# Softmax sums of the tokens as 128x8 distinct values, and an output projection split into 384 and 128 columns, in a recurrent-memory attention kernel

## The chip, the cores and the metric

The kernel runs on one core of a Trainium2 chip. A core has five engines with instruction queues of their own: TensorE (matrix products, PE in the profile; its weight loads are shown apart as PEld), VectorE (DVE), ScalarE (ACT), GpSimd (POOL) and SyncE (SP), which in this kernel only issues DMA transfers. Matrix products are written to PSUM, eight banks of 128 partitions by 512 fp32 values; everything else lives in SBUF or DRAM. The metric is the device time of one execution in microseconds, as the median of several runs. Beside it stands one profiled execution, from which all durations are read.

## The reference

A gated mix of two branches over 2048 tokens of width 512. Branch B is a layer norm with a two-layer MLP. Branch A is attention with a recurrent memory and is where the change lies: the tokens are cut into 64 segments of 32, and each segment is attended together with 8 memory rows, which the segment before has made.

```python
idx = jnp.arange(L)                                    # L = M + seg = 8 + 32
mask = (idx[:, None] < M) | (idx[:, None] >= idx[None, :])
mem = mem0
for s in range(n_seg):                                 # 64
    xs = x[:, s * seg_len:(s + 1) * seg_len, :]
    h = jnp.concatenate([mem, xs], axis=1)
    q = jnp.einsum('btd,dhe->bhte', h, Wq)             # 32 heads of 128
    k = jnp.einsum('btd,dhe->bhte', h, Wk)
    v = jnp.einsum('btd,dhe->bhte', h, Wv)
    scores = jnp.einsum('bhqe,bhke->bhqk', q, k) * scale
    p = _softmax(jnp.where(mask[None, None], scores, -1e9), axis=-1)
    o = jnp.einsum('bhqk,bhke->bhqe', p, v)
    o = jnp.einsum('bhte,hed->btd', o, Wo)
    mem = o[:, :M, :]
    outs.append(o[:, M:, :])
a = jnp.concatenate(outs, axis=1)
return g * a + (1 - g) * b                             # g = sigmoid((x * gate_w).sum(-1))
```

## The kernel before

The first 100 us run branch B over all tokens, keep its result `c` in DRAM and load the weights of branch A. Then 64 steps `s`, one per segment, run in an order written out by hand; every engine executes its queue in the order of the program. `T, si = divmod(s, 4)`: four segments make a tile of 128 tokens.

A step works on 32 rows, the 8 memory rows and the first 24 tokens of its segment (`hT`); the last 8 tokens of each segment (LEFT) don't depend on the memory as queries, keys and values, and are projected for a whole tile at a time, as side work. Products of 32 rows use a quarter of the array's columns, so four of them, at the four column tiles, run side by side.

What a step issues, in TensorE's order:

- q and k (L110, banks `U[0]` to `U[3]`; cast by ScalarE at L115, transposed by VectorE at L119), a mask added to the score banks `Sb[0]` (in bank `SbF`) and `Sb[1]` (in bank `W`) at L248, scores of heads 0 to 15 (L256, L260), v (L129, banks `X1`, `X2`), scores of heads 16 to 31.
- The exponentials (L661, ScalarE) write `E`: for each of 8 groups i of 4 heads, 56 columns per key row, of which 0 to 15 belong to the 8 memory queries (they come twice), 16 to 47 to the 32 token queries, and 48 to 55 to the left tokens' keys for the last 8 of these queries. The key rows of four heads j lie in four blocks of 32 partitions.
- The sums over keys for the memory queries (`msum`, L267 and L270), their reciprocal (L668) and the product with E (L669, VectorE, two SBUF operands) are needed at once: attention times V (`av`, L280 and L285) reads E after it, in two halves.
- The sums for the token queries (`sums` with `xsum`, L693): the ones-blocks `BO` are the weights and E moves, so that each sum comes out on 32 partitions alike, 256 columns in `SbF`.
- `recip_x` (L603): VectorE inverts those 256 columns; SP sends four partitions of them to DRAM (`r_dr`, L606) and reads them back onto all 128 partitions (`Rb`, L607, 4 KB per partition); GpSimd adds the inverse to a running check (`racc`, L608).
- After `av`, ScalarE copies the memory columns to `UT` (L697) and the unnormalized token columns to `XR` (L598). In the next step GpSimd multiplies `XR` by `Rb` (`x_norm`, L614 and L615) into the columns 8 to 31 of `UT` and into `UL`. So the tokens of a segment are projected one step later than its memory rows: `wo_pass` in step s projects the memory rows of s and the tokens of s - 1.
- `wo_pass` (L618): eight groups of four matmuls (L141, 512 columns) into bank `W`, then ScalarE's copy to `w` (L622). Then a mask (L248), some side work, and the four matmuls that pick and transpose the memory rows of `w` (L709, 128 columns of `w` each). VectorE copies them to the next step's `hT` (L710), and the next q and k wait for that.

`fill` is the side work, handed out in pieces of four matmuls by `run(n)`: two pieces before the token sums (W1), two after `av` (W2), two after `wo_pass` (W3), the rest after L709. By si it is the next tile's left q and k (0 and 1), the last tile's left output (2) or left v (3); `extra` adds an output selection for si 0 and a transposition for si 3, between W3 and L709. `flush` runs pending copies in VectorE's and ScalarE's queues.

GpSimd's queue in a step: the next `hT` copy (L239), `x_norm` of the step before (it waits for Rb), `racc`, `prep_q` (L243); once in four steps the copy `GL` (L163). SP's queue: the loads of `c`, `VP` and `xs`, the two transfers of `recip_x`, the output. After the loop, the last step's sums, projection and check.

Of the kernel before, what the change touches and what calls it, by code (L numbers as in the profile page):

```python
# [27 lines left out]
def kernel(ctx, tc, A_x, A_mem0, A_Wq, A_Wk, A_Wv, A_Wo, A_seg_len, B_x, B_w1, B_b1, B_w2, B_b2, gate_w, out):  # L28
# [36 lines left out]
    r_dr = [dram.tile([4, 32 * NG], FP32, name=f"r_dr{i}") for i in range(2)]  # L65
# [71 lines left out]
    def wo_group(bk, U_, n):  # L137
        j, ih = HORD[n]
        for c in range(4):
            i = 4 * ih + c  # L140
            nc.tensor.matmul(bk[32 * c:32 * c + 32, :], lhsT=U_[:, j, i, :], rhs=Wo_sb[:, 4 * i + j, :],  # L141
                             start=(n == 0), stop=(n == NW - 1), tile_position=(0, 32 * c))
# [451 lines left out]

    def x_raw(s):
# [5 lines left out]
    def recip_x(s):  # L601
        R = Rs.pop(s)
        nc.vector.reciprocal(out=R[:, 8 * NG:], in_=SbF[:, 0:32 * NG])  # L603

        Rb = cw.tile([P, 4, NG, 32], FP32, tag="Rb", bufs=1, name="Rb")
        nc.sync.dma_start(r_dr[s % 2][:], R[0:P:32, 8 * NG:])  # L606
        nc.sync.dma_start(Rb[:].rearrange("p j i q -> p (j i q)"), r_dr[s % 2][:].rearrange("j f -> (j f)").partition_broadcast(P))  # L607
        nc.gpsimd.tensor_tensor(out=racc[:], in0=racc[:], in1=R[:], op=ALU.add)  # L608
        Rbs[s] = Rb

    def x_norm(s):
        T, si = divmod(s, SPT)
        XR, Rb = XRs.pop(s)[:].rearrange("p j i q -> p (j i) q"), Rbs.pop(s)[:].rearrange("p j i q -> p (j i) q")
        nc.gpsimd.tensor_tensor(out=UT[(s + 1) % 2][:].rearrange("p j i q -> p (j i) q")[:, :, M:32], in0=XR[:, :, 0:RIDE], in1=Rb[:, :, 0:RIDE], op=ALU.mult)  # L614
        nc.gpsimd.tensor_tensor(out=UL[T % 2][:].rearrange("p j i q -> p (j i) q")[:, :, LEFT * si:LEFT * si + LEFT],  # L615
                                in0=XR[:, :, RIDE:32], in1=Rb[:, :, RIDE:32], op=ALU.mult)

    def wo_pass(U_):  # L618
        for n in range(NW):
            wo_group(W, U_, n)  # L620
        w = cw.tile([P, Dm], BF16, tag="w", bufs=8, name="w")
        nc.scalar.copy(out=w[:], in_=W[:])  # L622
        return w

    W1, W2, W3 = 2, 2, 2
    for s in range(nseg):
# [56 lines left out]
        for i2 in range(2):  # L683
            exps(1, i2)
        for kc in range(2, KC):
# [7 lines left out]
        sums(xsum, E, 16, 48, 32, True)  # L693
# [18 lines left out]
        nc.vector.tensor_tensor(out=rmin[:], in0=rmin[:], in1=R[:], op=ALU.min)  # L712
# [166 lines left out]
```

## Time and profile before

| what | us |
|---|---|
| median of 3 runs | 796.58 |
| lowest, highest run | 795.5, 797.68 |
| profiled execution | 799.87 |
| its span, from the first to the last record | 798.1 |
| TensorE busy in the span | 774.5 (97%) |
| ScalarE busy | 529.9 (66%) |
| VectorE busy | 444.0 (56%) |
| GpSimd busy | 260.4 (33%) |

The granted clock of TensorE was 0.999 of full speed. Rows of the grouped view read: line, engine, operation, output <- inputs, shapes, count | busy us, mean ns of one | idle time of the engine just before, with what ended it. Rows of a timeline read: start us, us, engine, line, operation, count, and in brackets the idle time before. Rows of the chain of work that ended last read: start us, us, what. Rows of the waits read: engine, line, tile <- what it waited for: us in total, times, longest. Matmuls are pipelined: a row's duration includes the tail of its last matmul (0.17 us), during which the next one already runs.

### The profile page before, as it was taken

To read this page: it belongs to the slowest core of one execution; us is meant where nothing else is said; L and a number is where in the kernel's file an instruction comes from. 1 tells how busy PE (TensorE), PEld (TensorE's weight loads), DVE (VectorE), ACT (ScalarE), POOL (GpSimd) and SP (SyncE) were. 2 spreads that over 40 slices of the span, in tenths; PEclk is the share of its full clock that TensorE was granted. 3 is DMA by queue.
4 is the path that set the end of the run, shared out by engine and by line. 5 is a ranking of instruction groups with operands and counts; after the bars stand their busy time and mean duration, and the time that the engine had idled before them with its cause. 6 is when DMAs were issued, how large, how long until landed. Compare 5 with 4: busy or idle time off the path is not lost.

```text
span 798.1 us, 41399 instructions
## 1 busy us (share of the span) xinstructions
PE 774.5 (97%) x18446; PEld 421.2 (53%) x18446; DVE 444.0 (56%) x1061; ACT 529.9 (66%) x1440; POOL 260.4 (33%) x391
## 2 busy tenths in 40 slices
PE   7999999999999999999999999999999999999996
PEld 5666554555555555555554555555555555555543
DVE  4776355555556454646555555655465556555554
ACT  3666676666666676666666667767666766666663
POOL 3111033333343333243343334333334333333331
PEclk9999999999999999999999999999999999999999
DMA  6779411212112222212121211222221212121211
GB/s 188 264 273 351 134 57 60 73 59 86 60 53 68 76 69 76 70 49 67 60 86 60 86 49 62 70 76 70 70 76 53 64 60 86 60 80 60 66 47 57
DMA packets 38151, 70.42 MB, mean 88 GB/s; under 512 B 3979, under 2 KB 27888, under 8 KB 36432
## 3 DMA queue, kind: packets, MB, share of 16 engines
q1 hardware_dynamic: 36448, 64.97, 24.5%
q8 instruction: 146, 2.39, 1.2%
q0 software_dynamic: 720, 1.97, 0.7%
q10 hardware_dynamic: 800, 0.79, 0.3%
q14 instruction: 37, 0.30, 0.1%
HBM read 59.06 MB, written 4.45 MB: 80 GB/s over the span
## 4 chain that ended last, share of the span: by engine, by line
PE 92%; ACT 3%; DVE 2%; issue 1%; DMA 1%; POOL 0%; DVEq 0%; POOLq 0%; ACTq 0%
PE U L110 28%; PE X L129 17%; PE W L141 14%; PE X L110 6%; PE U L468 5%; PE U L280 4%; PE X L141 3%; ACT w L622 3%; PE W L462 3%; PE SbF L462 3%; PE W L709 1%; PE U L267 1%; DVE E L669 1%; PE SbF L256 1%; PE W L248 1%
## 5 line engine op out<-in xcount | busy, mean ns | idle before, releaser
L115 ACT CAST Tb<-U 128x512 bf16<-128x512 f32 x258 | 151.2, 586 | 81.3 <-PE U L110 80.8
L614 POOL TENSOR_TENSOR UT<-XR,Rb 128x768 bf16<-128x768 bf16 x63 | 104.7, 1662 | 239.8 <-DMA Rb<-r_dr 214.6
L110 PEld LDWEIGHTS <-hT 128*32 128x32 bf16 x4096 | 103.7, 97 | 109.9 <-DVE hT L710 19.1
L110 PE MATMUL U<-Wq_sb,hT 128*32 128x512 bf16 x2048 | 132.7, 379 | 1.1 <-DVE hT L710 1.1
L129 PE MATMUL X<-Wv_sb,hT 128*32 128x512 bf16 x2048 | 133.5, 378 | 0.0
L110 PE MATMUL U<-Wk_sb,hT 128*32 128x512 bf16 x2048 | 132.7, 379 | 0.0
L141 PE MATMUL W<-Wo_sb,UT 128*32 128x512 bf16 x2080 | 124.3, 380 | 1.2 <-ACT UT L697 1.2
L608 POOL TENSOR_TENSOR racc<-racc,R 128x320 f32<-128x320 f32 x63 | 54.5, 866 | 181.1 <-DVE R L603 176.5
L603 DVE RECIPROCAL R<-SbF 128x256 f32<-128x256 f32 x63 | 110.3, 1751 | 0.0
L119 DVE STREAM_TRANSPOSE QT<-Tb 128x256 f32<-128x256 f32 x128 | 57.0, 446 | 74.2 <-ACT Tb L115 74.1
L119 DVE STREAM_TRANSPOSE KT<-Tb 128x256 f32<-128x256 f32 x128 | 57.0, 445 | 54.9 <-ACT Tb L115 54.9
L141 PEld LDWEIGHTS <-UT 128*32 128x32 bf16 x2080 | 56.3, 96 | 58.5 <-issue 20.0
L710 DVE CAST hT<-W 128x32 bf16<-128x32 f32 x63 | 12.1, 192 | 132.8 <-PE W L709 132.8
L598 ACT CAST XR<-U 128x256 bf16<-128x256 f32 x252 | 78.4, 434 | 0.0
L622 ACT CAST w<-W 128x512 bf16<-128x512 f32 x65 | 38.1, 586 | 44.8 <-PE W L141 44.8
L697 ACT CAST UT<-U 128x64 bf16<-128x64 f32 x252 | 35.3, 226 | 46.7 <-PE U L285 46.7
L668 DVE RECIPROCAL R<-U 128x32 f32<-128x32 f32 x126 | 44.9, 357 | 25.7 <-PE U L270 24.2
L129 PEld LDWEIGHTS <-hT 128*32 128x32 bf16 x2048 | 45.4, 95 | 20.6
L468 PE MATMUL U<-w_sb,hTm 128*128 128x512 bf16 (+1 forms) x176 | 53.0, 385 | 0.0
L115 ACT CAST Tb<-X 128x512 bf16<-128x512 f32 x62 | 36.5, 589 | 18.0 <-PE X L110 18.0
L462 PEld LDWEIGHTS <-w_sb 128*128 128x128 bf16 (+1 forms) x352 | 34.9, 102 | 21.4 <-issue 4.6
L267 PEld LDWEIGHTS <-BO 128*32 128x32 bf16 x760 | 26.9, 95 | 33.9 <-issue 14.5
(155 smaller groups left out, 1220.5 us busy)
## 6 DMA issues: line engine op xcount, KB each, us to landing
Rb<-r_dr SPq DMA_DIRECT2D x63, 512.0 KB
Wv_sb<-in_A_Wv_dram SPq DMA_DIRECT2D x4, 1024.0 KB
Wq_sb<-in_A_Wq_dram SPq DMA_DIRECT2D x4, 1024.0 KB
Wk_sb<-in_A_Wk_dram SPq DMA_DIRECT2D x4, 1024.0 KB
Wo_sb<-in_A_Wo_dram SPq DMA_DIRECT2D x4, 1024.0 KB
VP<-VL SPq DMA_DIRECT2D x64, 64.0 KB
xt<-in_A_x_dram SPq DMA_DIRECT2D x16, 128.0 KB
xs<-in_A_x_dram SPq DMA_DIRECT2D x16, 128.0 KB
```

Source lines behind the costliest of these rows:

```text
L110: nc.tensor.matmul(bk[32 * j:32 * j + 32, :], lhsT=G[:, kc, :], rhs=W5[t][:, kc, h0:h1, j, :], start=(kc == 0), stop=(kc == KC - 1), tile_ ...
L115: nc.scalar.copy(out=Tb[:], in_=bk.rearrange("p (a b e) -> p a e b", a=8, b=2))
L119: nc.vector.transpose(out=dst[:, 8 * hf:8 * hf + 8, 0:32, :].rearrange("p a r b -> p a (r b)").bitcast(FP32), in_=Tb[:].rearrange("p a e b ...
L129: nc.tensor.matmul(bk[32 * j:32 * j + 32, :], lhsT=G[:, kc, :], rhs=Wv5[:, kc, 4 * vb:4 * vb + 4, j, :], start=(kc == 0), stop=(kc == KC - ...
L141: nc.tensor.matmul(bk[32 * c:32 * c + 32, :], lhsT=U_[:, j, i, :], rhs=Wo_sb[:, 4 * i + j, :], start=(n == 0), stop=(n == NW - 1), tile_po ...
L462: nc.tensor.matmul(hp[:rows, 0:TB * P], lhsT=w1_sb[:, kc, fc * P:fc * P + rows], rhs=yTs[blk][:, kc, :], start=(kc == 0), stop=(kc == KC - 1))
L468: nc.tensor.matmul(bp(blk, tt)[:], lhsT=hTm[blk % 2][:rows, fc, tt * P:(tt + 1) * P], rhs=w2_sb[:rows, fc, :], start=(fc == 0), stop=(fc = ...
L598: nc.scalar.copy(out=XR[:, j], in_=U[j][:, 0:NG * 40].rearrange("p (i q) -> p i q", q=40)[:, :, 8:40])
L603: nc.vector.reciprocal(out=R[:, 8 * NG:], in_=SbF[:, 0:32 * NG])
L608: nc.gpsimd.tensor_tensor(out=racc[:], in0=racc[:], in1=R[:], op=ALU.add)
L614: nc.gpsimd.tensor_tensor(out=UT[(s + 1) % 2][:].rearrange("p j i q -> p (j i) q")[:, :, M:32], in0=XR[:, :, 0:RIDE], in1=Rb[:, :, 0:RIDE] ...
L622: nc.scalar.copy(out=w[:], in_=W[:])
```

## The change

Three edits in the loop, which belong to two matters.

The token sums are made the other way round: slices of E (and, for the left keys, of a zero-padded copy `EZ` of E's last columns) are the weights and one column of each ones-block moves, so that each sum comes out once: partition 32c + q, column 4h + j, with i = 4h + c. `recip_x` inverts 128x8 values, sends all 128 partitions (32 B of each) to DRAM and reads 4 KB back onto each partition as before, in another order. `x_norm` has to read that order, with four instructions instead of two. `racc` and `rmin` take 72 columns instead of 320.

`wo_pass` computes columns 0 to 383 in bank `W` and copies them on ScalarE, then columns 384 to 511 in bank `U[0]`, copied by VectorE.

```diff
-    r_dr = [dram.tile([4, 32 * NG], FP32, name=f"r_dr{i}") for i in range(2)]
+    r_dr = [dram.tile([P, NG], FP32, name=f"r_dr{i}") for i in range(2)]
...
-    def wo_group(bk, U_, n):
+    def wo_group(bk, U_, n, d=slice(0, 512)):
...
-            nc.tensor.matmul(bk[32 * c:32 * c + 32, :], lhsT=U_[:, j, i, :], rhs=Wo_sb[:, 4 * i + j, :],
+            nc.tensor.matmul(bk[32 * c:32 * c + 32, 0:d.stop - d.start], lhsT=U_[:, j, i, :], rhs=Wo_sb[:, 4 * i + j, d],
...
+    xs8 = SbF[:, 256:256 + NG]
+    RW = 9 * NG
+    EZ = [lp.tile([P, NG, 32], BF16, name=f"EZ{i}") for i in range(2)]
+    for i in range(2):
+        nc.gpsimd.memset(EZ[i][:, :, 0:RIDE], 0.0)
+
+    def xsums(s, E):
+        for first, src, c0 in ((True, E, 16), (False, EZ[s % 2], 0)):
+            for i in range(NG):
+                c, h = i % 4, i // 4
+                nc.tensor.matmul(xs8[32 * c:32 * c + 32, 4 * h:4 * h + 4], lhsT=src[:, i, c0:c0 + 32], rhs=BO[:, 0:P:32],
+                                 start=first and h == 0, stop=not first, skip_group_check=True, tile_position=(0, 32 * c))
...
-        nc.vector.reciprocal(out=R[:, 8 * NG:], in_=SbF[:, 0:32 * NG])
+        nc.vector.reciprocal(out=R[:, 8 * NG:RW], in_=xs8)
-        Rb = cw.tile([P, 4, NG, 32], FP32, tag="Rb", bufs=1, name="Rb")
-        nc.sync.dma_start(r_dr[s % 2][:], R[0:P:32, 8 * NG:])
-        nc.sync.dma_start(Rb[:].rearrange("p j i q -> p (j i q)"), r_dr[s % 2][:].rearrange("j f -> (j f)").partition_broadcast(P))
-        nc.gpsimd.tensor_tensor(out=racc[:], in0=racc[:], in1=R[:], op=ALU.add)
+        Rb = cw.tile([P, P, NG], FP32, tag="Rb", bufs=1, name="Rb")
+        nc.sync.dma_start(r_dr[s % 2][:], R[:, 8 * NG:RW])
+        nc.sync.dma_start(Rb[:].rearrange("p r e -> p (r e)"), r_dr[s % 2][:].rearrange("r e -> (r e)").partition_broadcast(P))
+        nc.gpsimd.tensor_tensor(out=racc[:, 0:RW], in0=racc[:, 0:RW], in1=R[:, 0:RW], op=ALU.add)
...
-        XR, Rb = XRs.pop(s)[:].rearrange("p j i q -> p (j i) q"), Rbs.pop(s)[:].rearrange("p j i q -> p (j i) q")
-        nc.gpsimd.tensor_tensor(out=UT[(s + 1) % 2][:].rearrange("p j i q -> p (j i) q")[:, :, M:32], in0=XR[:, :, 0:RIDE], in1=Rb[:, :, 0:RIDE], op=ALU.mult)
-        nc.gpsimd.tensor_tensor(out=UL[T % 2][:].rearrange("p j i q -> p (j i) q")[:, :, LEFT * si:LEFT * si + LEFT],
-                                in0=XR[:, :, RIDE:32], in1=Rb[:, :, RIDE:32], op=ALU.mult)
+        XR, Rb = XRs.pop(s), Rbs.pop(s)[:].rearrange("p (c q) (h j) -> p h j c q", c=4, h=2)
+        for out, o, a, b in ((UT[(s + 1) % 2], M, 0, RIDE), (UL[T % 2], LEFT * si, RIDE, 32)):
+            for h in range(2):
+                nc.gpsimd.tensor_tensor(out=out[:, :, 4 * h:4 * h + 4, o:o + b - a], in0=XR[:, :, 4 * h:4 * h + 4, a:b], in1=Rb[:, h, :, :, a:b], op=ALU.mult)
...
     def wo_pass(U_):
-        for n in range(NW):
-            wo_group(W, U_, n)
         w = cw.tile([P, Dm], BF16, tag="w", bufs=8, name="w")
-        nc.scalar.copy(out=w[:], in_=W[:])
+        for bk, d, copy in ((W, slice(0, 384), nc.scalar.copy), (U[0], slice(384, Dm), nc.vector.tensor_copy)):
+            for n in range(NW):
+                wo_group(bk, U_, n, d)
+            copy(out=w[:, d], in_=bk[:, 0:d.stop - d.start])
         return w
...
             exps(1, i2)
+        if not last:
+            nc.scalar.copy(out=EZ[s % 2][:, :, RIDE:32], in_=E[:, :, 48:56])
...
-        sums(xsum, E, 16, 48, 32, True)
+        xsums(s, E)
...
-        nc.vector.tensor_tensor(out=rmin[:], in0=rmin[:], in1=R[:], op=ALU.min)
+        nc.vector.tensor_tensor(out=rmin[:, 0:RW], in0=rmin[:, 0:RW], in1=R[:, 0:RW], op=ALU.min)
```

In the last step the token sums stay as they were.

## The prediction

> **What bounds the kernel now.** I read the page's chain of work first, then the chain piece by piece through the 63 steps that end in the memory projection, then the timeline of single steps.
>
> ```profile
> PE 92%; ACT 3%; DVE 2%; issue 1%; DMA 1%; POOL 0%; DVEq 0%; POOLq 0%; ACTq 0%
> ```
>
> TensorE carries the chain. Two engines own what is left of it, and each is one place of the loop. The first is ScalarE's copy of the projected row block `w` (L622). Waits, then the chain at one of those places, then TensorE's own timeline there:
>
> ```profile
> PEld L709 <- ACT w L622: 23.8, 36, 1.0
> ...
> PE W L709 <- ACT w L622: 6.3, 34, 0.6
> ```
> ```profile
> 421.49 0.02 issue
> 421.51 0.59 ACT w L622
> 422.10 0.05 issue
> 422.15 0.26 PE W L709 x4
> ```
> ```profile
> 419.55 1.91 PE L141 MATMUL W<-Wo_sb,UT 128*32 128x512 bf16 x32
> 421.28 0.28 PE L248 MATMUL SbF<-Mk,ident 128*32 128x224 bf16 x4
> 421.37 0.62 PE L110 MATMUL X<-Wk_sb,GL 128*32 128x512 bf16 x8
> 422.15 0.26 PE L709 MATMUL W<-SelM,w 128*128 128x8 bf16 x4 [0.16 <-ACT w L622]
> ```
>
> After the projection TensorE has 0.09 us of mask and eight matmuls (two groups of 0.215, priced below) as cover; that ends about 421.80. The row selection (L709) starts at 422.15, so the array stands for 0.35 us. The 0.16 in the row is smaller because the tail of the last matmul still counts as busy. The piecewise chain has this copy in 35 of the 63 steps (the rows above count 36 and 34): the steps with si 1 and 2, and the first and last ones. In the other 28 the transposes or the output selection lie in between, and L709 starts as soon as `w` is there:
>
> ```profile
> 400.01 0.59 ACT L622 CAST w<-W 128x512 bf16<-128x512 f32 x1 [0.65 <-PE W L141]
> ...
> 400.66 0.25 PE L709 MATMUL W<-SelM,w 128*128 128x8 bf16 x4
> ...
> 401.01 0.19 DVE L710 CAST hT<-W 128x32 bf16<-128x32 f32 x1 [2.05 <-PE W L709]
> ```
>
> The second place is VectorE's small product at L669, in an ordinary step and in a bad one:
>
> ```profile
> 404.51 1.66 POOL L614 TENSOR_TENSOR UT<-XR,Rb 128x768 bf16<-128x768 bf16 x1 [2.16 <-DMA Rb<-r_dr]
> ...
> 406.84 0.23 DVE L669 TENSOR_TENSOR E<-E,R 128x64 bf16<-128x64 bf16 x1
> 407.25 0.36 DVE L668 RECIPROCAL R<-U 128x32 f32<-128x32 f32 x1 [0.18 <-PE U L270]
> ```
> ```profile
> 232.34 1.66 POOL L614 TENSOR_TENSOR UT<-XR,Rb 128x768 bf16<-128x768 bf16 x1 [3.97 <-DMA Rb<-r_dr]
> ```
> ```profile
> 232.87 1.22 DVE L669 TENSOR_TENSOR E<-E,R 128x64 bf16<-128x64 bf16 x1
> ```
>
> When GpSimd's normalization is under way as L669 comes up, L669 lasts until that instruction ends (232.34 + 1.66 = 234.00; 232.87 + 1.22 = 234.09). Its mean over 126 is 287 ns instead of 230, some 7 us of blocking; 0.18 us of each block is free (407.25 less 407.07). Four steps with blocks of 1 us and more, and a handful of half-blocked ones, lengthen their steps by about 4 us in this execution.
>
> **The change, part by part.**
>
> *Output projection.* The prices:
>
> ```profile
> L622 ACT CAST w<-W 128x512 bf16<-128x512 f32 x65 | 38.1, 586 | 44.8 <-PE W L141 44.8
> ...
> L669 DVE TENSOR_TENSOR E<-E,R 128x64 bf16<-128x64 bf16 x126 | 36.2, 287 | 13.5 <-ACT V L687 0.5
> ...
> L710 DVE CAST hT<-W 128x32 bf16<-128x32 f32 x63 | 12.1, 192 | 132.8 <-PE W L709 132.8
> ...
> L731 DVE CAST UT<-U 128x256 bf16<-128x256 f32 x2 | 0.8, 420 | 0.6 <-PE U L285 0.6
> ...
> L731 ACT CAST UT<-U 128x256 bf16<-128x256 f32 x2 | 0.6, 375 | 0.2 <-PE U L285 0.2
> ```
>
> ScalarE's 384 columns lie halfway between 375 and 586 ns: 0.48. VectorE's 128 columns, between 192 and 420: 0.29. The W bank is complete 0.45 us before the pass ends, so ScalarE's part is done 0.05 after the pass; `x_raw` ahead of it is through by then. VectorE's part ends last: after the pass, a short matmul's tail (0.17), about 0.08 to react, 0.29, and 0.05 to TensorE, against 0.17 + 0.02 + 0.59 + 0.05 = 0.83 now. So 0.59 after the pass instead of 0.83, with TensorE's cover at 0.52; only the fourth selection matmul needs VectorE's columns, some 0.06 later than the first. The stall falls from 0.35 to nearly nothing. VectorE's queue is empty there because the long reciprocal goes; with it (until 409.60 in the row below) the copy would still start in time.
>
> TensorE's cost, from the chain:
>
> ```profile
> 400.82 0.08 PE W L709 x4
> ...
> 402.41 2.59 PE U L110 x48
> 405.00 0.10 PE SbF L256 x16
> ...
> 407.63 0.11 PE SbF L267 x4
> 407.74 0.03 PE SbF L270 x4
> ```
>
> A group of four with 512 columns takes 2.59 / 12 = 0.216 us (512 columns at 0.417 ns are 0.213, so 2 to 3 ns per group on top). Sixteen pairs of weights and 40 columns take 0.10, four groups at 25 ns where columns alone are 17: at most 8 ns on top. Eight more groups per pass cost 0.02 to 0.07 us; I take 0.04. Lower bound of nothing: the columns are the same.
>
> Per step: with cover, 0.35 - 0.02 - 0.04 = 0.29 gained in 32; in the 3 with none, 0.83 - 0.59 - 0.04 = 0.20; in the other 28, 0.04 lost; the tail's last pass gains 0.2. Together -9.3 - 0.6 + 1.1 - 0.2 = **-9.0 us**. With the VectorE part anywhere from 0.25 to 0.42 and the groups from 0.02 to 0.07 it is -11 to -4.
>
> *Token sums.* 4 + 4 matmuls (0.11 + 0.03) become 16 pairs with 4 columns, nearest to L256's 16 pairs: 0.10. Neither sign reaches the end, because what follows waits elsewhere:
>
> ```profile
> 406.69 0.42 ACT L661 ACTIVATE E<-W 128x64 bf16<-128x64 f32 x2
> ...
> 407.08 0.59 ACT L687 CAST V<-X 128x512 bf16<-128x512 f32 x1
> ...
> 407.71 0.23 DVE L669 TENSOR_TENSOR E<-E,R 128x64 bf16<-128x64 bf16 x1
> ...
> 407.85 1.75 DVE L603 RECIPROCAL R<-SbF 128x256 f32<-128x256 f32 x1
> ...
> 407.99 0.28 PE L280 MATMUL U<-E,V 32*128 32x40 bf16 x16
> ```
>
> The second half of attention times V starts at 407.99, right behind the second L669 (407.94), and not behind the sums; a tenth of a microsecond more in them is hidden. The new copy of E's last columns into `EZ` stands on ScalarE between the exponentials (end 407.11) and the copy of V. At about 0.2 us it moves V's end from 407.67 to some 407.9, still behind L669's cover; bounds 0 and 0.06 per step. I take 0. Queued behind it are only V's copy and, through it, that second half.
>
> *Reciprocal and its way through DRAM.* 256 values take 1.75 us; 8 are nearest to L668's 32 in 0.36, so 0.2. The two DMAs issue about 1.5 us earlier on SP, ahead of the same output store as before; the loads they had to share with come later. The first writes 128 pieces of 32 B instead of 4 of 1 KB: now 1.1 us a time from the row below; I allow up to 0.5 more. Rb's landing is seen by L614, at 3.5 after the previous L710 (401.01) ordinarily; I expect 1.9 to 2.5. `racc` and `rmin` shrink from 320 to 72 columns, off the path.
>
> ```profile
> SPq L607 <- DMA r_dr<-R: 69.4, 63, 1.9
> ```
>
> *Normalization on GpSimd.* Two instructions become four of 384, 384, 128 and 128 elements, whose Rb operand steps 32 B.
>
> ```profile
> L614 POOL TENSOR_TENSOR UT<-XR,Rb 128x768 bf16<-128x768 bf16 x63 | 104.7, 1662 | 239.8 <-DMA Rb<-r_dr 214.6 <-ACT Tb L115 25.3
> ...
> L615 POOL TENSOR_TENSOR UL<-XR,Rb 128x256 bf16<-128x256 bf16 x63 | 42.6, 676 | 0.0
> ...
> L243 POOL COPY QT<-QL 128x128 f32<-128x128 f32 x64 | 26.6, 415 | 0.0
> ...
> L239 POOL COPY hT<-xT 128x96 bf16<-128x96 bf16 x64 | 17.3, 270 | 0.0
> ...
> L163 POOL COPY GL<-xT 128x128 bf16<-128x128 bf16 x16 | 10.2, 648 | 17.9 <-DVE xT L160 17.8
> ```
>
> L614 and L615 give 1.9 ns per element and 0.18 fixed. Without any cost of stride the four take 2.7 us. L243 reads with a step of 16 B and is 55 ns dearer than L239 scaled to 128 elements (360), 0.4 ns per element; L163 writes with a step of 8 B and is 290 dearer, 2.3 per element. Over 1024 elements: 2.7, 3.1 or 5.0 us. A read is nearest to L243: **3.1**, from about 2.1 to 5.2 after L710. L669 comes up at 5.83 (406.84 less 401.01). So the four blocks of 1 us go and most half-blocks too, while a late Rb now and then still meets the last piece (0.4 us): -4 + 0.6 = **-3.4**.
>
> The Trainium skill speaks against this part: in "GPSIMD Engine Reference", section 7 (performance pitfalls), a read whose step exceeds 8 bytes costs about 2.9 instead of 1.9 cycles per element. By it, as an estimate, one cycle more at that page's 1.2 GHz is 0.85 us over 1024 elements, 3.6 us in all, and the normalization would end near 5.7, against 5.83: hardly a margin. L243's surplus is half of that.
>
> **Sum.** The profiled execution took 799.87 us (span 798.1 and 1.8 around it): 799.87 - 9.0 - 3.4 = 787.5. The median of the plain runs is 796.58, 3.3 less, perhaps because Rb was late less often in them; then 796.58 - 9.0 with a collision term of -0.5 is 787.1. I predict **787.3**, and 783 to 792 as this case's own range.
>
> **The rivals.**
>
> 1. *Slower: the normalization meets L669 in every step.* If strided reads cost what L163's strided writes do (5.0 us) and Rb lands at 2.4, the pieces end at 4.2, 6.0, 6.7 and 7.4. The first L669 (5.83) waits for the second piece and the second L669 for the last two; less the free 0.18, about 0.4 per step, 25 us over 63: **812**. It decides from an end of the pieces past 6.0 after L710. For: L163, and blocks already seen. Against: L243, and Rb's earlier start. The Trainium skill, "SBUF — State Buffer", section "Who interferes with whom", says that a VectorE instruction with two SBUF inputs contends with a GpSimd one that reads SBUF and the later one waits out the whole instruction; the block at 232.87 agrees.
>
> 2. *Slower: short matmuls are bound by their number.* L709's four run at 0.02 us each. At that rate 32 matmuls of 128 columns take 0.68 instead of 0.43 and the 16 sums 0.34: +0.25 per pass over the 0.04, +0.08 past the cover of the sums. 65 x 0.25 + 63 x 0.08 = 21 us: **808**. It decides where a pass grows by more than 0.2. Against: L256's 16 pairs in 0.10, in the same four column tiles. "TensorE: Matmul & The Clock Gate" of the Trainium skill (section on back-to-back issue) gives a floor of about 25 ns per small matmul, which would make the pass still longer; L256's 6 ns each contradict it in these tiles.
>
> 3. *Little gained: VectorE's copy is as late as ScalarE's was.* If 128 columns cost what 256 do (0.42) and the reaction is 0.13, `w` is ready 0.77 after the pass: 0.06 less 0.04 gained in 35 steps, 0.04 lost in 28, the collisions a little better: **795**. For: L731's 420. Against: 192 for 32 columns.
>
> **How the numbers follow.** Chances: forecast 0.66, rival 1 0.13, rival 2 0.08, rival 3 0.13. Against 796.58, 0.3% is 2.4 us, about what this measurement tells from none. Faster takes the forecast and half of rival 3, 0.72; same 0.07; slower rivals 1 and 2, 0.21. The range of 782 to 805 holds the forecast and rival 3 whole, and the milder ends of the other two.
>
> **What would show it.** L709 with no wait for L622 in steps with si 1 and 2, and their length 0.3 shorter; the two passes of L141 together 1.75 to 1.8 us; L669 at 0.23 throughout; the first normalization near 2 after L710 and the last ended before 5.8; the sums within 0.12; V's copy ending before the second L669. Wrong would be: pieces longer than 1.3 us each, a pass above 1.95, VectorE's copy above 0.4, or a new wait of L280 for V.

## The result, and the profile after

The changed kernel takes 800.54 us (median of 8 runs, 797.89 to 802.36) beside 796.75 of the kernel before in the same comparison (8 runs, 795.5 to 798.1). The ratio is 1.0052, 95% interval 1.0038 to 1.0065: slower by half a per cent, where 787.3 was forecast. The profiled execution took 799.8 us with a span of 798.0 and a granted clock of 0.997, against 799.87 and 798.1 before. So the trace of before shows an execution 3.1 us above its median, that of after one 0.7 below.

First the page of the kernel after (busy times, two DMA queues, the chain by engine), then the same rows of before as far as they were not shown.

```profile
PE 771.5 (97%) x21001; PEld 462.7 (58%) x21030; DVE 345.2 (43%) x1126; ACT 533.6 (67%) x1503; POOL 277.4 (35%) x519
...
q8 instruction: 166, 2.72, 1.4%
...
PE 95%; issue 2%; ACT 1%; DMA 1%; DVE 0%; POOL 0%; SPq 0%; DVEq 0%; POOLq 0%; ACTq 0%
```
```profile
PE 774.5 (97%) x18446; PEld 421.2 (53%) x18446; DVE 444.0 (56%) x1061; ACT 529.9 (66%) x1440; POOL 260.4 (33%) x391
...
q8 instruction: 146, 2.39, 1.2%
```

ScalarE fell from 3% of the chain to 1%, VectorE from 2% to nothing: both waits that the prediction went after are mostly gone. In their place "issue" rose from 1% to 2%: time in which TensorE stands and the profile shows nothing that it waits for. The instruction queue q8 says where to look: 20 more packets of 16 KB. TensorE has 21,001 + 21,030 - 2 x 18,446 = 5,139 more records, 257 for each of these packets, so I take a packet for a block of 256 instructions of 64 B.

The terms of the sum, by groups of the kernel after:

```profile
L629 POOL TENSOR_TENSOR UT<-XR,Rb 128x384 bf16<-128x384 bf16 x126 | 139.9, 1133 | 259.5 <-DMA Rb<-r_dr 191.8
...
L637 DVE CAST w<-U 128x128 bf16<-128x128 f32 x65 | 19.0, 292 | 180.0 <-ACT w L637 172.6
...
L629 POOL TENSOR_TENSOR UL<-XR,Rb 128x128 bf16<-128x128 bf16 x126 | 60.6, 504 | 0.0
...
L637 ACT CAST w<-W 128x384 bf16<-128x384 f32 x65 | 31.2, 480 | 20.6 <-PE W L141 20.6
```
```profile
L684 DVE TENSOR_TENSOR E<-E,R 128x64 bf16<-128x64 bf16 x126 | 30.9, 245 | 13.5 <-ACT E L676 0.5
...
L616 DVE RECIPROCAL R<-SbF 128x8 f32<-128x8 f32 x63 | 12.6, 201 | 0.0
```
```profile
L701 ACT COPY EZ<-E 128x64 bf16<-128x64 bf16 x63 | 15.4, 244 | 2.0
```

Sizes were right: the copies of `w` 0.48 and 0.29, the reciprocal 0.20, the normalization 2 x 1.133 + 2 x 0.504 = 3.27 (3.1 taken), the small product (L684, before L669) down from 287 to 245 ns. The timeline of the same step as in the prediction, now from its L727 (before L710):

```profile
399.51 0.19 DVE L727 CAST hT<-W 128x32 bf16<-128x32 f32 x1 [0.64 <-PE W L726]
...
401.47 2.23 POOL L629 TENSOR_TENSOR UT<-XR,Rb 128x384 bf16<-128x384 bf16 x2 [0.82 <-ACT Tb L115]
403.65 0.95 POOL L629 TENSOR_TENSOR UL<-XR,Rb 128x128 bf16<-128x128 bf16 x2
...
405.34 0.23 DVE L684 TENSOR_TENSOR E<-E,R 128x64 bf16<-128x64 bf16 x1
```

The normalization begins 1.96 after L727 and ends 5.09 after it; the product comes at 5.83 and finds the way free. At the projection of a step with si 1:

```profile
506.28 0.63 PE L141 MATMUL U<-Wo_sb,UT 128*32 128x128 bf16 x32
506.52 0.48 ACT L637 CAST w<-W 128x384 bf16<-128x384 f32 x1 [0.22 <-PE W L141]
...
506.82 0.62 PE L110 MATMUL X<-Wk_sb,GL 128*32 128x512 bf16 x8
...
507.03 0.29 DVE L637 CAST w<-U 128x128 bf16<-128x128 f32 x1 [2.69 <-ACT w L637]
...
507.37 0.17 PEld L726 LDWEIGHTS <-w 128*128 128x128 bf16 x4 [0.42 <-ACT w L637]
507.38 0.26 PE L726 MATMUL W<-SelM,w 128*128 128x8 bf16 x4
```

The eight matmuls of cover end at about 507.25 (506.82 and two groups of 0.215), L726 (before L709) starts at 507.38: the array stands for 0.13 instead of 0.35. The first selection waits for ScalarE's part alone, which is done at 507.00, so I read that remainder as the way from column tiles to the whole array rather than as a wait for `w`. VectorE's copy ends at 507.32, just ahead of L726, and could be suspected too; but in three steps (at 150.28, 173.07 and 724.37 us) it is done 0.16 to 0.58 us ahead, and L726 still starts 0.31 to 0.32 us after the start of the last matmul before it, as here.

So where did the time go? I measured each step from row selection to row selection and took, for each si, the third shortest of the loop as its undisturbed length. Four steps took 10.64 + 10.65 + 10.65 + 10.86 = 42.80 us before and 10.43 + 10.44 + 10.68 + 10.88 = 42.43 after. That is 0.37 per tile, 6 us over the 16 tiles, gained. What the steps took beyond these lengths grew from 5.0 to 11.8 us and ate it. The chain of waits of the kernel after shows one such place, in a second half of attention times V:

```profile
470.96 0.10 PE SbF L605 x15
471.06 0.21 PE U L280 x16
471.27 0.03 PE U L285 x4
471.31 0.02 issue
471.33 0.23 PE U L280 x9
471.56 0.70 issue
472.26 0.22 PE U L280 x7
```

TensorE stops within one line, after 9 of 16 equal matmuls, and goes on 0.7 us later. No operand is late: the other seven read the same V and E. Such stops come in L280, L285, L141, L110, alike only in their numbers. Counted from the trace's first TensorE record, the stops that follow the starts at 158.51, 280.74, 449.10 and 471.39 us come before the records 5,044, 12,209, 22,190 and 23,469; modulo 256 these are 180, 177, 174 and 173 (a slow drift, since a few instructions leave no record). They are the ends of the blocks of q8. I call what TensorE loses there **waits at block ends**: pauses over 225 ns from the start of one of its records to the start of the next at these numbers, each less the 216 ns that a group of four matmuls with 512 columns takes anyway, from 115 to 740 us. There are 5 with 1.1 us before and 29 with 7.7 us after.

A block's packet starts 0.95 us after TensorE has entered the block ahead of it (median of those outside Rb's transfer), lasts 1.1, and in the stops above TensorE went on 1.2 to 1.5 us after its end: some 3.5 us for a block when nothing was fetched ahead. The densest 256 instructions took at least 3.08 us without their stops before, and 2.72 after. The Trainium skill, "Runtime: NRT & Kernel Launch", section "Instruction fetch mechanics", describes the blocks of 16 KiB and has their cost hidden because dispatch is slower than the fill; here, in a stretch of small matmuls, it is the other way round.

### The profile page after: what moved, and what is told of

Same layout as the page of the kernel before. It is cut to its first block, busy times and chain, and to the rows that moved or that the text cites. A ratio compares the mean times of both kernels' runs of the same rounds, so it can differ in the third digit from the quotient of the medians.

```text
span 798.0 us, 46764 instructions
## 1 busy us (share of the span) xinstructions
PE 771.5 (97%) x21001; PEld 462.7 (58%) x21030; DVE 345.2 (43%) x1126; ACT 533.6 (67%) x1503; POOL 277.4 (35%) x519
## 3 DMA queue, kind: packets, MB, share of 16 engines
q8 instruction: 166, 2.72, 1.4%
## 4 chain that ended last, share of the span: by engine, by line
PE 95%; issue 2%; ACT 1%; DMA 1%; DVE 0%; POOL 0%; SPq 0%; DVEq 0%; POOLq 0%; ACTq 0%
PE U L110 28%; PE X L129 18%; PE W L141 11%; PE X L110 8%; PE U L468 5%; PE U L280 4%; PE X L141 4%; PE U L141 4%; PE W L462 3%; PE SbF L462 3%; PE W L726 1%; PE U L267 1%; PE SbF L256 1%; PE SbF L605 1%; PE W L256 1%
## 5 line engine op out<-in xcount | busy, mean ns | idle before, releaser
L629 POOL TENSOR_TENSOR UT<-XR,Rb 128x384 bf16<-128x384 bf16 x126 | 139.9, 1133 | 259.5 <-DMA Rb<-r_dr 191.8
L110 PEld LDWEIGHTS <-hT 128*32 128x32 bf16 x4096 | 105.9, 97 | 108.4 <-DVE hT L727 18.5
L110 PE MATMUL U<-Wq_sb,hT 128*32 128x512 bf16 x2048 | 134.0, 379 | 1.2 <-DVE hT L727 1.1
L110 PE MATMUL U<-Wk_sb,hT 128*32 128x512 bf16 x2048 | 133.8, 379 | 0.0
L141 PEld LDWEIGHTS <-UT 128*32 128x32 bf16 x4160 | 94.7, 96 | 45.4 <-POOL racc L621 17.2
L141 PE MATMUL W<-Wo_sb,UT 128*32 128x384 bf16 x2080 | 98.1, 327 | 2.3 <-ACT UT L714 1.4
L637 DVE CAST w<-U 128x128 bf16<-128x128 f32 x65 | 19.0, 292 | 180.0 <-ACT w L637 172.6
L621 POOL TENSOR_TENSOR racc<-racc,R 128x72 f32<-128x72 f32 x63 | 21.2, 337 | 113.9 <-DVE R L616 111.3
L629 POOL TENSOR_TENSOR UL<-XR,Rb 128x128 bf16<-128x128 bf16 x126 | 60.6, 504 | 0.0
L129 PEld LDWEIGHTS <-hT 128*32 128x32 bf16 x2048 | 47.4, 95 | 19.9 <-issue 0.4
L468 PE MATMUL U<-w_sb,hTm 128*128 128x512 bf16 (+1 forms) x163 | 49.4, 380 | 0.6
L637 ACT CAST w<-W 128x384 bf16<-128x384 f32 x65 | 31.2, 480 | 20.6 <-PE W L141 20.6
L256 PEld LDWEIGHTS <-KT 128*32 128x32 bf16 x2048 | 34.8, 95 | 16.2 <-issue 0.3
```

The source lines that it names most:

```text
L110: nc.tensor.matmul(bk[32 * j:32 * j + 32, :], lhsT=G[:, kc, :], rhs=W5[t][:, kc, h0:h1, j, :], start=(kc == 0), stop=(kc == KC - 1), tile_ ...
L129: nc.tensor.matmul(bk[32 * j:32 * j + 32, :], lhsT=G[:, kc, :], rhs=Wv5[:, kc, 4 * vb:4 * vb + 4, j, :], start=(kc == 0), stop=(kc == KC - ...
L141: nc.tensor.matmul(bk[32 * c:32 * c + 32, 0:d.stop - d.start], lhsT=U_[:, j, i, :], rhs=Wo_sb[:, 4 * i + j, d], start=(n == 0), stop=(n == ...
L256: nc.tensor.matmul(Sb[i2][32 * j:32 * j + 32, i - 4 * i2, M:M + 40], lhsT=KT[:, h // 2, :, h % 2], rhs=QT[:, h // 2, :, h % 2], start=Fals ...
L468: nc.tensor.matmul(bp(blk, tt)[:], lhsT=hTm[blk % 2][:rows, fc, tt * P:(tt + 1) * P], rhs=w2_sb[:rows, fc, :], start=(fc == 0), stop=(fc = ...
L629: nc.gpsimd.tensor_tensor(out=out[:, :, 4 * h:4 * h + 4, o:o + b - a], in0=XR[:, :, 4 * h:4 * h + 4, a:b], in1=Rb[:, h, :, :, a:b], op=ALU ...
```

## The experiments

All runs below compare with the kernel before on the same chip at the same time (medians 795.66 to 796.42). For reading along, the measured numbers of all; "tile" is the undisturbed length of four steps, "fetch" the median time from entering a block to the start of the next one's packet, for packets that start while Rb is being moved / for the others. Tile, waits and fetch are read from one profiled execution of each kernel, and that can lie off the median: 3.3 us below it for late_recip, 2.6 for idle_mid, 1.9 for half_rb, 1.5 above it for shift_q.

```
kernel         records  median us  ratio [95% interval]      tile   waits at     fetch us
               per tile                                      us     block ends   in Rb / else
before           2230    796.75     1                         42.80   5, 1.1 us   0.90 / 1.02
after            2549    800.54     1.0052 [1.0038, 1.0065]   42.43  29, 7.7      2.86 / 0.95
sums_only        2294    795.90     1.0000 [0.9988, 1.0012]   42.80   4, 0.8      1.68 / 0.93
wo_only          2486    791.93     0.9953 [0.9940, 0.9966]   42.42   0, 0.0      1.37 / 1.05
halves           2486    799.52     1.0053 [1.0041, 1.0066]   42.89   1, 0.3
copy_split       2294    806.34     1.0139 [1.0123, 1.0154]   43.44   6, 0.8
pairs_dense      2549    792.20     0.9959 [0.9946, 0.9973]   42.42  16, 1.7      0.86 / 0.96
pairs_sparse     2549    794.28     0.9983 [0.9971, 0.9994]   42.63   3, 0.4      0.58 / 0.80
shift            2549    796.71     1.0011 [0.9998, 1.0023]   42.41  15, 2.2      2.62 / 0.81
shift_q          2549    795.73     0.9996 [0.9985, 1.0006]   42.43  24, 3.7      2.48 / 0.92
sums_ten         2501    791.52     0.9951 [0.9933, 0.9969]   42.42  12, 1.6      2.41 / 0.81
no_rb            2549    790.65     0.9926 [0.9911, 0.9941]   42.42  10, 1.2         - / 0.77
half_rb          2549    795.46     0.9997 [0.9982, 1.0012]   42.43  17, 2.2
ten_half         2501    793.39     0.9966 [0.9953, 0.9980]   42.41  15, 2.4
pairs_rb         2549    824.51     1.0342 [1.0322, 1.0362]   43.10  11, 2.5
idle_rb          2549    794.74     0.9993 [0.9979, 1.0008]   42.42  17, 3.3      2.64 / 0.83
idle_late        2549    798.34     1.0025 [1.0009, 1.0041]   42.43  29, 6.3      1.49 / 1.04
idle_mid         2549    798.74     1.0023 [1.0006, 1.0040]   42.43  22, 3.9      1.78 / 1.02
late_recip       2549    812.26     1.0202 [1.0188, 1.0216]   42.67  10, 1.3
pairs_store      2549    793.89     0.9972 [0.9959, 0.9985]   42.41   8, 0.7      0.77 / 0.87
```

### Each half of the change alone

sums_only has the new token sums and the old projection (of the change's diff, all but the hunk of `wo_pass`), wo_only the reverse (the hunks of `wo_group` and `wo_pass` alone). halves is the kernel before with each projection matmul cut in two:

```diff
-        for n in range(NW):
-            wo_group(W, U_, n)
+        for d in (slice(0, 256), slice(256, Dm)):
+            for n in range(NW):
+                wo_group(W, U_, n, d, d)
```

copy_split has the new sums and one pass of 512 columns, copied by both engines:

```diff
-        nc.scalar.copy(out=w[:], in_=W[:])
+        nc.scalar.copy(out=w[:, 0:320], in_=W[:, 0:320])
+        nc.vector.tensor_copy(out=w[:, 320:Dm], in_=W[:, 320:Dm])
```

> The token sums as changed, the projection as before (one pass of 512 columns, one copy by ScalarE). Two theories of why the changed kernel gave back its gain. Supply: TensorE runs out of instructions in its dense stretch, because the split pass adds 64 instructions per step; the new sums add only 16. Then this kernel has few waits of TensorE with no releaser, and without the long blocks of the small product by GpSimd it stands at 794 to 797 us, against 796.75 before. Transfers: the 128 small pieces of the first DMA and the earlier second one hold up what TensorE waits for; then the waits stay as in the changed kernel, and with no shorter way for w it is slower than it: 803 to 807.

> The projection split into 384 and 128 columns as changed, the token sums as before. Supply: 64 instructions more per step bring the waits of TensorE at every 256th instruction; the shorter way of w gains 6 to 7 us and the waits take 5 to 9 back: 795 to 799. Transfers: with the old DMAs there are no such waits and the gain of w shows whole: 789 to 791.

> The kernel before, with each projection matmul of 512 columns cut into two of 256 in the same bank: 64 instructions more per step, the same columns, the same single copy by ScalarE. Supply: 1 us for the additional matmuls and 5 to 9 us of waits at every 256th instruction: 802 to 807. Transfers: only the 1 to 2 us for the matmuls: 798 to 799.

> The token sums as changed; the projection in one pass of 512 columns as before, but w copied from the one bank by two engines, 320 columns by ScalarE and 192 by VectorE. Supply: nearly all of the shorter way of w without the 64 instructions; w is ready about 0.47 instead of 0.66 us after the pass, 0.18 less in 35 steps, 6 us, and few waits: 788 to 792. Transfers: the waits stay, 797 to 801.

The new sums alone cost and gain nothing (795.90), so the theory that their transfers slow the kernel by themselves falls. The split alone gives 791.93, between the ranges of the two theories: it **beats both kernels**, its tile is as short as the changed kernel's, and it has no wait at a block end. One half is worth +0.2, the other -3.7; both together are worth +3.8. The loss is a meeting of the two. halves prices the further instructions: the tile grows by 0.09, 0.02 per pass, the low end of the prediction's 0.02 to 0.07. Its median, 799.52, lies above what Transfers had and below what Supply had. It is 3.9 above before, of which 16 x 0.09 = 1.4 is explained by that and the rest isn't: the trace has one wait at a block end, 0.3 us.

copy_split missed both ranges for a reason of its own. Its groups:

```profile
L636 DVE CAST w<-W 128x192 bf16<-128x192 f32 x65 | 23.2, 357 | 195.3 <-ACT w L635 195.3
...
L635 ACT CAST w<-W 128x320 bf16<-128x320 f32 x65 | 27.6, 425 | 44.5 <-PE W L141 44.5
```

VectorE's copy waits for ScalarE's every time: in the program it carries a wait on that engine, since both write the tile `w`. So they run one after the other, 0.425 + 0.357 instead of 0.586, and every step takes 10.86. The changed kernel has this wait too (172.6 us in L637's row above), though its two copies read different banks; there it costs little, because ScalarE's part is done as the second bank is.

### How many instructions, and where

Idle pairs are a weight load and a matmul with 4 columns whose results nobody reads:

```diff
+    def pairs(bk, n):
+        for i in range(n):
+            c = i % 4
+            nc.tensor.matmul(bk[32 * c:32 * c + 32, 0:4], lhsT=BO[:, 32 * c:32 * c + 32], rhs=BO[:, 0:P:32],
+                             start=True, stop=True, skip_group_check=True, tile_position=(0, 32 * c))
```

In pairs_dense (on wo_only), pairs_sparse (on wo_only) and shift (on the changed kernel, ahead of the loop) they are issued so:

```diff
         sums(xsum, E, 16, 48, 32, True)
+        pairs(W, 8)
...
                 qk_unit(bk, hc, t, hf, kc)
+                if n == 2 and kc in (0, 2):
+                    pairs(U[3], 4)
...
     W1, W2, W3 = 2, 2, 2
+    pairs(U[3], 64)
```

sums_ten is the changed kernel with the second half of its sums in two matmuls over the whole array:

```diff
-        for first, src, c0 in ((True, E, 16), (False, EZ[s % 2], 0)):
...
+        for h in range(2):
+            nc.tensor.matmul(xs8[:, 4 * h:4 * h + 4], lhsT=EZ[s % 2][:, 4 * h:4 * h + 4, :], rhs=BO[:, 0:P:32],
+                             start=False, stop=True, skip_group_check=True)
```

> The kernel with only the split projection (791.9), plus eight idle pairs of weights and 4 columns right behind the old token sums, so that TensorE gets as many instructions per step as in the changed kernel, at the same place, while the sums, the reciprocal and the two transfers stay the old ones. Their results are read by nobody. Theory Supply (256 instructions may not pass in less than about 3.3 us): waits at block ends return, 798 to 802. Theory Meeting (the waits need the new sums' own work: the scattered store of r_dr, GpSimd's four pieces): 791.5 to 793.

> The same eight pairs per step on top of the split projection, but four and four between the K projection's groups of 512 columns, where 256 instructions take far longer than 3.3 us. Nothing covers them there: 63 x 0.05 = 3 us of matmul time. Theory Supply: no more than these 3 us, 794 to 796, and few waits at block ends, which makes it faster than pairs_dense by 4 us or more. Theory Meeting: 794 to 796 too, but slower than pairs_dense by about 2.

> The changed kernel with 64 idle pairs (128 instructions, half a block of 256, about 0.4 us) ahead of the loop, so that every block end falls half a block earlier in each step. Theory Supply by density alone: the same waits at other places, 799 to 802. Theory Position (the waits are many because the block ends happen to fall at bad places in this kernel): 792 to 797.

> The changed kernel with its 16 pairs of token sums made in ten: the main half as before in eight column-tiled pairs, the half over EZ in two pairs with 128 stationary columns. The computation is whole; 12 instructions fewer per step than the changed kernel, 4 more than the split projection alone; the transfers and GpSimd's four pieces stay the new ones. Theory Supply: 790 to 795. Theory Meeting: 798 to 801.

pairs_dense has the changed kernel's number of instructions at every point and is as dense (256 in 2.76 us at the least), and takes 792.20. So the number alone doesn't do it, against the theory Supply. sums_ten has the new transfers and takes 791.52, the lowest time of a whole kernel here, no further from wo_only than the spread of either; with 12 instructions fewer per step its densest 256 take 2.99 us. So the new sums' transfers don't do it alone either. shift moves every block end by half a block and gains 3.8; the place of the block ends counts too. pairs_sparse is dearer than pairs_dense, by its uncovered matmul time (0.21 per tile).

### With and without the broadcast

What the changed kernel has and pairs_dense has not is Rb's transfer, 512 KB, at another place: its first packet leaves 0.6 us ahead of the row selection (median), before the change 1.0 after it. In the changed kernel the 39 block packets that start during that transfer do so 2.86 us after TensorE entered the block ahead, the 106 others 0.95. No block's packet starts between 0.4 and 1.6 us after Rb's first packet. no_rb leaves the broadcast out:

```diff
-        nc.sync.dma_start(Rb[:].rearrange("p r e -> p (r e)"), r_dr[s % 2][:].rearrange("r e -> (r e)").partition_broadcast(P))
-        Rbs[s] = Rb
+        Rbs[s] = Rc
```

half_rb casts the reciprocals to bf16 first (`r_dr` and `Rb` become bf16 too); ten_half does so in sums_ten. pairs_rb adds an idle store and broadcast to pairs_dense:

```diff
+        Rh = cw.tile([P, NG], BF16, tag="Rh", name="Rh")
+        nc.vector.tensor_copy(out=Rh[:], in_=R[:, 8 * NG:RW])
-        nc.sync.dma_start(r_dr[s % 2][:], R[:, 8 * NG:RW])
+        nc.sync.dma_start(r_dr[s % 2][:], Rh[:])
```
```diff
         pairs(W, 8)
+        nc.sync.dma_start(x_dr[s % 2][:], R[:, 32:40])
+        Rx = cw.tile([P, P * NG], FP32, tag="Rx", bufs=1, name="Rx")
+        nc.sync.dma_start(Rx[:], x_dr[s % 2][:].rearrange("r e -> (r e)").partition_broadcast(P))
         recip_x(s)
```

> The changed kernel with the broadcast of Rb (512 KB, 128 pieces of 4 KB) left out of the loop: GpSimd multiplies by a constant tile instead of the reciprocals, so the walkers' tokens are scaled by 0.01. TensorE's instructions, their number and their places stay. Theory Broadcast (a block of 256 instructions that is fetched while Rb is being moved comes about 2 us later, and the next dense stretch has no lead left): the waits at block ends go, 790 to 793. Theory Density (the number of instructions in the dense stretch and where the block ends fall are enough): 798 to 802.

> The changed kernel with the reciprocals cast to bf16 ahead of the store, so that r_dr and Rb have half the bytes (pieces of 2 KB, some 1.3 us instead of 2.6 on the way). The computation is whole. One more VectorE cast of 8 columns. Theory Broadcast: about half the waits, 793 to 797. Theory Density: 798 to 802.

> Token sums in ten pairs (791.5 alone) and the broadcast halved as in half_rb. The computation is whole. Theory Broadcast: the rest of the waits at block ends shrinks, 788.5 to 791. Theory Density: as sums_ten, 790.5 to 793.

> The reverse: pairs_dense (792.2; split projection, old sums, eight idle pairs, so the changed kernel's number of instructions at every point) plus an idle store and broadcast of the size of r_dr and Rb, issued where the changed kernel issues its own; nobody reads it, and the old Rb follows behind it. Theory Broadcast: the waits at block ends appear, 796 to 803. Theory Density: 791.5 to 793.5.

no_rb takes 790.65, 9.9 us under the changed kernel, with the same TensorE instructions at the same numbers. Up to 2.5 of the 9.9 are not TensorE's stops: VectorE's small product is no longer blocked (225 ns in the mean of 126, after 245). The place shown above, in its chain of waits:

```profile
466.06 0.10 PE SbF L607 x15
466.16 0.21 PE U L280 x16
466.37 0.03 PE U L285 x4
466.41 0.02 issue
466.43 0.40 PE U L280 x16
```

Sixteen matmuls in one piece. half_rb keeps about half of the loss, as expected, but its cast also moved the transfer: Rb leaves about 0.4 after the row selection, so amount and place changed together. ten_half missed both ranges: 793.39, no better than sums_ten (791.52, intervals overlapping). Halving the bytes did not help where the demand was already lower.

pairs_rb lost far more than either theory had, and elsewhere. Its old Rb now queues behind the idle one, and the normalization comes late; a step of it, and the group:

```profile
226.64 1.65 POOL L615 TENSOR_TENSOR UT<-XR,Rb 128x768 bf16<-128x768 bf16 x1 [6.05 <-DMA Rb<-r_dr]
226.69 1.68 DVE L678 TENSOR_TENSOR E<-E,R 128x64 bf16<-128x64 bf16 x1
```
```profile
L678 DVE TENSOR_TENSOR E<-E,R 128x64 bf16<-128x64 bf16 x126 | 67.9, 539 | 13.2
```

That is the collision with VectorE's small product, at 539 ns in the mean; of the block ends this run says nothing.

### Transfer, readers, place

With no_rb went the transfer and GpSimd's waiting for it. idle_rb has the transfer back with no reader (GpSimd multiplies by the constant). idle_late sends it one hop later:

```diff
+        nc.sync.dma_start(q_dr[s % 2][:], r_dr[s % 2][:])
-        nc.sync.dma_start(Rb[:].rearrange("p r e -> p (r e)"), r_dr[s % 2][:].rearrange("r e -> (r e)").partition_broadcast(P))
+        nc.sync.dma_start(Rb[:].rearrange("p r e -> p (r e)"), q_dr[s % 2][:].rearrange("r e -> (r e)").partition_broadcast(P))
```

idle_mid is idle_rb, and late_recip the changed kernel, with an idle reciprocal ahead of the short one, so that Rb goes out where it did before:

```diff
+        Ri = cw.tile([P, 248], FP32, tag="Ri", bufs=1, name="Ri")
+        nc.vector.reciprocal(out=Ri[:], in_=rmin[:, RW:])
         nc.vector.reciprocal(out=R[:, 8 * NG:RW], in_=xs8)
```

shift_q is shift with 32 pairs. pairs_store is pairs_dense with an idle store in 128 pieces of 32 B behind r_dr:

```diff
         nc.sync.dma_start(r_dr[s % 2][:], R[0:P:32, 8 * NG:])
+        nc.sync.dma_start(x_dr[s % 2][:], R[:, 32:40])
```

> no_rb with the broadcast put back and read by nobody: Rb is moved in the changed kernel's place, while GpSimd still multiplies by the constant tile (the walkers' tokens are scaled by 0.01). Theory Broadcast: the transfer alone brings the waits at block ends back, 796 to 801. Theory Readers (what went with no_rb was GpSimd's waiting for Rb and its later pieces, not the transfer): 790 to 792.

> As idle_rb, with one more hop of 4 KB through DRAM between r_dr and the broadcast, so that the idle Rb is moved about 2 us later in the step, near where the kernel before moves it. Theory Broadcast: it is the place of the transfer in the step that counts, so fewer waits, 791 to 796 and at least 3 us under idle_rb. If it is the amount that is moved and not the place: within 1.5 us of idle_rb. Theory Readers: 790 to 792.

> idle_rb (broadcast read by nobody, constant multiplier) with an idle reciprocal of 248 columns on VectorE ahead of the short one, so that r_dr and the idle Rb go out about 1.6 us later, where the kernel before has them (Rb begins 1.0 us after the row selection instead of 0.7 ahead of it; in idle_late it was 1.95 after). Theory Place: it is where the transfer stands against the blocks of 256, and the old place is a good one here, as in pairs_dense: 791 to 793. Theory Amount: as idle_rb or between it and idle_late, 794 to 799.

> The changed kernel, whole, with the same idle reciprocal ahead of the short one: Rb back in its old place. Theory Place: most waits at block ends go (7.7 us), but GpSimd's four pieces end 1.6 us later and meet VectorE's product again as in the kernel before or worse (+3 to +8): 793 to 801. Theory Amount: waits stay and the blocks come on top, 803 to 809.

> The changed kernel with 32 idle pairs (64 instructions, a quarter of a block) ahead of the loop; with 64 pairs it took 796.7, with none 800.5. Theory Place: another relation of transfer and block ends, another time, anywhere from 792 to 802 and not forecast. If the number of instructions in the dense stretch decided alone: 799 to 802.

> pairs_dense (792.2: the changed kernel's number of TensorE instructions, old sums, old r_dr of 4 pieces of 1 KB, broadcast in the old place) with an idle store of 128 pieces of 32 B, the size of the changed kernel's r_dr, between r_dr and the broadcast; nobody reads it. Theory Store: the scattered store together with the broadcast makes the waits at block ends that idle_mid had and pairs_dense had not: 795 to 800. Theory Position: the store does nothing, 791.5 to 793.5, and what parts idle_mid from pairs_dense lies in where the requests of the blocks fall.

The transfer alone, read by nobody, costs 4.1 us over no_rb (794.74, between the ranges of the two theories), and the waits at block ends rise from 10 with 1.2 us to 17 with 3.3. So the transfer is a cause, and not the whole loss: from idle_rb to the changed kernel it is another 5.8. In the traces 4.4 of that are waits at block ends (3.3 and 7.7), and up to 2.4 are blocks of VectorE's small product (226 and 245 ns in the mean of 126). A later place does not help, against my theory: 798.34, which no theory had, and 798.74, both dearer than idle_rb. In all three the tile is 42.42 to 42.43, so what differs is the stops. shift_q agrees with shift: of three positions of the block ends the change as made has the worst one, 800.54 beside 796.71 and 795.73. The scattered store does about 1.7 us (793.89, between the two ranges and with an interval that overlaps that of pairs_dense), so it isn't what parts idle_mid, 4.9 higher, from pairs_dense.

late_recip shows what the short reciprocal is worth. Its group of the small product:

```profile
L686 DVE TENSOR_TENSOR E<-E,R 128x64 bf16<-128x64 bf16 x126 | 58.7, 466 | 13.1
```

With Rb 1.6 us later GpSimd's four pieces meet the product in most steps (466 ns in the mean, 94 of 126 blocked) and the kernel takes 812.26, above both ranges. The four pieces can be afforded only because the reciprocal became short; the same earlier Rb then meets TensorE's blocks.

## Why the prediction was wrong

**The step that failed** is the price of the further TensorE instructions: "Eight more groups per pass cost 0.02 to 0.07 us", and of the sums "Neither sign reaches the end". As matmul time both hold (halves 0.02 per pass, sums_only 1.0000). But 2,549 instead of 2,230 instructions per tile also have to be fetched, and the sum had no term for that: +6.6 us of waits at block ends. With it went the sentence that the earlier DMAs only move ("the loads they had to share with come later"): the broadcast shares with the instruction blocks as well. Either alone was harmless, and the edits were costed one by one. Without its waits the changed kernel would have stood near 793 (800.54 - 7.7, an estimate), at the upper end of the forecast's range of 783 to 792; the rest of the miss lies mainly in the terms below that were too large.

- *Projection, -9.0.* Right in kind, too large: undisturbed steps gained 6 us. "The stall falls from 0.35 to nearly nothing" became 0.13, and steps with si 1 and 2 are 0.21 shorter, not 0.29: the sum had nothing for the way from column tiles to the whole array. The covered steps lost 0.02 to 0.03 (0.04 taken). VectorE's copy does wait for ScalarE's, which the text did not see; it cost next to nothing here.
- *Sums and EZ copy, 0.* Right for themselves (795.90 for the sums alone).
- *Normalization, -3.4.* The mechanism held to a tenth of a microsecond (3.27 us, ended 5.09 after L727), but the money was not there: sums_only has these pieces and is no faster. The 4 us of blocking belonged to a profiled execution 3.3 us above the median. The second way of the sum, with 0.5, was the better one.
- *Sum.* By the profiled executions: 799.87 - 6.0 + (11.8 - 5.0) = 800.7, measured 799.8. The medians differ by +3.8 all the same, because the profiled execution of before lies 3.1 above its median and that of after 0.7 below.
- *Rivals.* Rival 1 did not happen (245 ns), but late_recip shows its price once Rb is late: 812.26, where the rival had 812. That the totals agree is luck: there the pieces take 3.3 us in all and start late, where the rival had pieces of 5.0. Rival 2 had the right suspect, the number of short matmuls, and the wrong mechanism: the array is not slower per matmul, and a pass grew by 0.02 us only. Rival 3 did not happen: 292 ns.
- *What would show it.* The normalization and the sums came out as listed; the steps were shorter by less (0.21 of 0.3), and L684 was at 245 ns in the mean, better than 287 but not at 0.23 throughout. None of the listed signs looked at "issue".

**What stays open.** Shown: neither the dense stretch without the broadcast (no_rb, 1.2 us of waits) nor the broadcast with a less dense stretch (sums_ten, 1.6) does much, and both together cost 7.7 with Rb and the block ends where the change has them (2.2 and 3.7 with the ends moved, 1.7 in pairs_dense with Rb elsewhere); the transfer alone accounts for 4.1 us in time.

How the two meet can be read at the changed kernel's 15 stops over 0.2 us, 6.4 us together. At the same 15 block ends no_rb, with the same TensorE instructions, stops for 0.09 us at most. In 11 of the 15 a packet started during Rb's transfer, in the block that the stop ends or in the one ahead of it; 70 of all 144 blocks have that. In nine of them the packet in the block ahead came 2.5 to 3.5 us after TensorE had entered that block, beside 0.6 to 1.2 in no_rb. So at these nine the delayed fetch did use up the lead with which TensorE enters the dense stretch: its next packet started 0.9 to 1.5 us into the stretch, and in no_rb earlier, three times already in the block ahead. In two more it was the packet of the ending block itself that came late, 3.5 and 3.75 us after entry; for the other four of the 15 neither is shown. idle_late, with its later broadcast, has the same picture at other blocks (12 of its 13 stops over 0.2 us, beside 58 of 144 blocks).

Open: why idle_mid has twice the waits of pairs_dense with the same instruction numbers and Rb at the same place, why the waits of idle_late are more than those of idle_rb, and why the waits rise from 3.3 to 7.7 us when GpSimd reads Rb.

## What to carry to other kernels

Count an engine's instructions, not only their time: where 256 of them pass in under about 3.5 us (the estimate from this case's packets), the fetch of the next block can end last, and a change that adds short matmuls there pays in stops with no releaser, at record numbers 256 apart. Two edits that each cost nothing can share one resource, so price the sum of their instructions and transfers too, and run each half alone: here the half (791.93) or the same sums in ten pairs (791.52) gains what the whole change loses. And don't bank on blocks seen in an execution that lies above the median.

## What the runs showed of the hardware

- TensorE's stops at block ends: up to 0.70 us of idle time each (at 471.56), 29 in the loop of the changed kernel.
- In the changed kernel a block's packet starts 2.86 us after the block ahead was entered if Rb's 512 KB are on their way, 0.95 otherwise; in pairs_dense, with Rb at another place of the step, 0.86 and 0.96.
- Moving all block ends by a quarter or half a block changes the time by 4.8 or 3.8 us, at the same work.
- Between matmuls in column tiles and L726 over the whole array 0.13 us passed (507.25 to 507.38) with the first operand there since 507.00; in three steps in which VectorE's part of `w` was ready 0.16 to 0.58 us ahead of L726, the way was as long.
